# A one-core attention and MLP block: the q weights loaded behind the second chunk of x, two statistics moved ahead, later K products in half rounds, and a new order of the work

## The chip, the cores and the metric

The kernel runs on one core of a Trainium2 chip. The metric is the device time of one execution in microseconds; lower is better. The time before the change is the median of three runs. One further execution was recorded by the profiler, and every duration below comes from that one. The engines are PE (matrix products), ACT, DVE and POOL (elementwise work), and SP, which here only issues transfers.

## The reference

One input x of 2048 rows by 512 columns is normalised per row. From the normalised x an attention with 32 query heads of width 16 and one shared key and value head is computed, and beside it an MLP; the result is x plus their product.

```python
xn = layernorm(x)                              # no scale, no shift, eps 1e-5
q = (xn @ wq) in 32 heads of 16; k = xn @ wk; v = xn @ wv      # one k, one v for all heads
p = softmax(q @ k.T / 4)
s = (p @ v, heads side by side) @ wo
g = silu(silu(xn @ w1) @ w2)                   # w1: 512 x 1792, w2: 1792 x 512
return x + s * g
```

All arrays are bfloat16. B_x is not used.

## The kernel before, in words

The kernel text does not list its instructions. It holds a planner (class Planner) that is run while the program is built: each piece of work is a task or a job with an estimated duration, the planner keeps a clock for each engine, and it places at every step the piece that can start with the best priority. The order so found is the order of each engine's queue; semaphores keep the dependences. On the chip every engine then works through its queue in that order, so an instruction that must wait holds up all that stands behind it.

The rows of x are 16 tiles of 128 rows, in four chunks of four tiles. All times of the planner are in nanoseconds.

**The start.** SP and ACT issue the loads of tiles 0 to 3 one by one, then SP issues wk, wv, wq (512 KB) and the second, third and fourth chunk of x (512 KB each), L482 to L490, in that order. DVE computes the statistics of a tile (L575), gathers them (L579), and writes the normalised tile (L611); ACT does the statistics of tile 1. PE transposes the normalised tile (L650), ACT or DVE copies the transposed tile out of PSUM (L660, L661). In the first chunk the K product (L685) and the first q product (L797) follow tile by tile, then the values (L723). For tiles 4 to 7 the statistics may only be placed once the copy of the transposed tile 3 has been placed (the gate at L578); the statistics of tiles 4 to 11 come together into one group of eight for the reciprocal root (FIRST = (2, 2, 8, 4)). The load of w1 (1792 KB) is issued by SP when tile 5's normalisation has been placed.

**Scores and exponentials.** 32 groups (16 blocks of heads, two halves of each) by 64 score tiles are 2,048 score products (L1033, L1039). Each is four matmuls of 64 rows by 32 columns with 512 moving columns. A score tile goes to one of two places: ACT takes the exponential (L1829, one or two tiles at a time, into pa_sb), or DVE makes an integer in 16 bits that stands for an exponential (L1124, into db_sb), of which POOL makes three shifted copies in batches of eight (L1311, into ds_sb). A tile of ACT needs one product with v, a tile of DVE needs four (L1393). DVE's share may begin only when the keys of 12 tiles are there (DK = 12).

**PE's two lanes.** Most work on PE is done in half rounds: four matmuls of 64 rows, which use half of the array, on lane 0 or lane 1; two half rounds run side by side. Scores, products with v, and the products of the MLP, q and the output (L761) are of this kind (mode "U"). A job of several half rounds does those of one lane first, then those of the other, and all sum into one bank of PSUM. Transposes, values and the K products are full rounds, which use both lanes: mode "F" is a full array, mode "C" four column groups with all 128 rows. A change of mode costs SWITCH = 105 in the plan. The K product of a chunk is four rounds of mode "C" (mk_K); with KU set to 1, a K product of a whole chunk is made a job of half rounds instead:

```python
if KU and n == NQ:
    product(jb, lambda k, rows, a, n: wk2(k, rows), lambda k, rows: xnT_sb[rows, k, ka * P:kb * P],
            lambda k: ["wk", "wv"] + keys)
```

In the main step (pe_step) a half round of a K job goes ahead of scores; on lane 0 other jobs go ahead of products with v, on lane 1 scores go first.

**The price of a transfer.** In Planner.place a load is taken to begin 1.85 us (early) or 1.4 us after its issue, or when the one before is through, to need its bytes divided by 250 per nanosecond, and 0.6 us more.

**The seeds.** The class Mix changes some twenty of the planner's thresholds at random for every 6 us of the plan, by the number that stands for that stretch in SEEDS; 0 keeps the base values. Another list of seeds gives another order of the whole middle. The end (the last output rows) has an order of its own.

Of the kernel before, what the change touches and what calls it, by code (L numbers as in the profile page):

```python
# [15 lines left out]
P = 128  # L16
DH = 16
# [2 lines left out]
W1_AT, SKIP = 5, 1877.999  # L20
T_ISSUE, T_SWDGE = 450.0, 1000.0
J_BASE, J_END, MIXJ = 0.114, 1.312, 2
SEEDS, STRETCH = [0, 621430, 964855, 634377, 64350, 0, 694092, 944034, 510981, 983451, 126593, 580856, 234150, 0, 405364, 0, 0, 639952, 236919, 380010, 794098, 385191, 672036, 0, 789095, 553358, 196796, 902258, 0, 0, 0, 514317, 0, 331162, 593301, 0, 0, 437315, 0, 0, 917832, 457243, 378342, 445316, 218187, 875070, 402692, 608418, 665513, 0, 0, 713570, 834070, 919202, 142859, 159991, 0, 53048, 725479, 111780, 0, 961704, 55976, 234814, 688798, 646486, 6388, 105124, 192922, 681295, 882883, 467008, 979031, 477536, 901050, 975096, 0, 0, 980853, 663567, 0, 620538, 913744, 251242, 618568, 299334, 120371, 0, 397467, 0, 362185, 47491, 718084, 0, 0, 0, 0, 0, 635882, 0, 0, 0, 0, 0, 0, 0, 0, 0, 0], 6000.0
STG = {2: 3, 3: 11}
LOG2E = 1.4426950408889634

# [12 lines left out]
T_TP, T_COLD, N_COLD = 46.0, 427.0, 11  # L39

KA = 0.0
T_V, T_VE, V_KB = 220.0, 410.0, 150

FIRST = (2, 2, 8, 4)
KU, VG_PRIO, ROOM0 = 0, 0, 4
T_SP, T_ST = 600.0, 480.0
FS, T_SQ, T_LD, PR_LD = 4, 210.0, 1500.0, 1

SHIFT = (0.0, 32.0, 64.0, 96.0)
# [4 lines left out]
PE, AC, DV, PO, SP = "PE", "ACT", "DVE", "POOL", "SP"  # L54
# [54 lines left out]
class Planner:  # L109
# [47 lines left out]
    def place(self, eng, dur, emit, reads, writes, dma=0, t0=None, ports=1, after=None):  # L157
        op = Op()
        op.eng, op.emit, op.inc, op.val, op.know, op.sem, op.ports = eng, emit, False, 0, None, None, ports
        deps = self.deps(eng, reads, writes)  # L160
        if after is not None:
            deps.append(after)
        other = self.last2.get(PO if eng == DV else DV) if ports == 2 and eng in self.last2 else None
        if other is not None:
            deps.append(other)
        seen = set()
        op.deps = []
        for d in deps:
            if id(d) not in seen:
                seen.add(id(d))  # L170
                op.deps.append(d)
        if t0 is None:
            t0 = max(self.clk[eng], self.ready(eng, reads, writes), self.locked(eng, ports))
        op.t0 = t0
        op.end = t0 + dur
        if eng in self.last2 and ports == 2:
            self.last2[eng] = op
        op.dma, op.ring = dma, None
        if dma < 0:
            op.vis = self.acc_t = max(op.end - dma, self.acc_t + ACC_GAP)  # L180
        elif dma:
            start = max(t0 + (1850.0 if t0 < 1000.0 else 1400.0), self.dma_t if dma > 1 else 0.0)
            if dma > 1:
                self.dma_t = start + dma / 250.0
            op.vis = start + dma / 250.0 + 600.0
        self.clk[eng] = op.end
        op.idx = len(self.order[eng])
        self.order[eng].append(op)
        self.count += 1
        for k in reads:  # L190
            self.readers.setdefault(k, []).append(op)
        for k in writes:
            self.lastw[k] = op
            self.readers[k] = []
        return op
# [179 lines left out]
def bass_recurrent_scan__grouped_kv_mqa__dense_activation_silu__prompt_kernel(  # L375
# [29 lines left out]
    with ExitStack() as es:  # L405
        def sb(name, shape, dt):
            return es.enter_context(nc.sbuf_tensor(name, shape, dt))
# [3 lines left out]
        wq_sb = sb("wq_sb", [P, NDC, D], BF16)  # L411
        wkv_sb = sb("wkv_sb", [P, NDC, 2 * DH], BF16)
# [39 lines left out]
        def x_tile(t):  # L452
            return ds_sb[:, XB + t // BS, (t % BS) * NQ:(t % BS + 1) * NQ].bitcast(BF16)
# [10 lines left out]
        pl = Planner()  # L464
# [8 lines left out]
        def dma(eng, name, out_, in_, kb, writes, reads=(), prio=1, preds=(), on_place=None):  # L473
            return pl.add(Task(eng, T_ISSUE, lambda e: e.dma_start(out_, in_), reads, writes, prio, preds, on_place,  # L474
                               dma=kb * 1024))

        def xkey(t):
            return ("Ds", XB + t // BS, t % BS)
# [3 lines left out]

        for t in range(4):
            dma((SP, AC)[t % 2], "x", x_tile(t), xv[:, t, :], 128, [xkey(t)], prio=-2)
        dma(SP, "wk", wkv_sb[:, :, 0:DH], A_wk.rearrange("(dc p) e -> p dc e", p=P), 16, ["wk"], prio=0)
        dma(SP, "wv", wkv_sb[:, :, DH:2 * DH], A_wv.rearrange("(dc p) e -> p dc e", p=P), 16, ["wv"], prio=0)
        dma(SP, "wq", wq_sb[:], A_wq.rearrange("(dc p) n -> p dc n", p=P), 512, ["wq"], prio=0)
        for j in range(1, 4):
            dma(SP, "x", ds_sb[:, XB + 4 * j // BS, 4 * j % BS * NQ:(4 * j % BS + 4) * NQ].bitcast(BF16).rearrange("p (t d) -> p t d", d=D),
                xv[:, 4 * j:4 * j + 4, :], 512, [xkey(4 * j + h) for h in range(4)], prio=1)  # L490
        def later(task, which):
# [69 lines left out]
        xn_task, t_done = {}, set()  # L561
# [9 lines left out]
        for j in range(4):  # L571
            for t in range(4 * j, 4 * j + 4):
                if t == 1:
                    continue
                ts_ = pl.add(Task(DV, 593.0, lambda v, t=t: v.bn_stats(stats_sb[:, t, :], x_tile(t)),  # L575
                                  [xkey(t)], [("st", t)], 1 + j,
                                  gate=(lambda j=j: xn_task[STG[j]].op is not None) if j > 1 else
                                  (lambda: ("xnT", 3) in pl.lastw) if j > 0 else None))  # L578
                pl.add(Task(DV, 66.0, lambda v, t=t: v.bn_aggr(mv_sb[:, t, :], stats_sb[:, t, :]),  # L579
                            [("st", t)], [("mv", t)], 1 + j, [ts_]))  # L580
        aggr = {w[1]: task for e in (DV, AC) for task in pl.tasks[e] for w in task.writes if isinstance(w, tuple) and w[0] == "mv"}
# [2 lines left out]
        for n in first:  # L584
# [5 lines left out]
            def dv(fn, reads, writes, pre, ports=1):  # L590
                return pl.add(Task(DV, 66.0, fn, reads, writes, g, [pre] if pre is not None else [], ports=ports))
            if a < FS:
                t = pl.add(Task(AC, T_SQ, lambda q, w=w, a=a, b=b: q.activation(w, mv_sb[:, a:b, 1], ACT.Sqrt, bias=scr_sb[:, 3:4]),
                                [("mv", i) for i in tiles] + ["eps"], [("ve", a)], -1, [aggr[i] for i in tiles] + [eps]))
                if b >= FS:
                    pl.add(Task(AC, T_LD, lambda q: q.activation(scr_sb[:, 0:1], scr_sb[:, 1:2], ACT.Exp), ["scr"], ["scr2"], PR_LD, [t]))
                t = dv(lambda v, y=y, w=w: v.reciprocal(y, w), [("ve", a)], [("rs", a)], t)
            else:
                t = pl.add(Task(DV, 66.0, lambda v, a=a, b=b, w=w: v.tensor_scalar(
                    w, mv_sb[:, a:b, 1], LN_EPS, None, op0=ALU.add), [("mv", i) for i in tiles], [("ve", a)], g,  # L600
                    [aggr[i] for i in tiles], ports=2))
                t = dv(lambda v, y=y, w=w: v.tensor_scalar(
                    y.bitcast(I32), w.bitcast(I32), -0.5, RSQRT_M, op0=ALU.mult, op1=ALU.add), [("ve", a)], [("rs", a)], t, 2)
                for it, (c0, c1) in enumerate(RSQRT_C):
                    t = dv(lambda v, y=y, h=h, c0=c0: v.scalar_tensor_tensor(
                        out=h, in0=y, scalar=c0, in1=y, op0=ALU.mult, op1=ALU.mult), [("rs", a)], [("vh", a)], t)
                    t = dv(lambda v, w=w, h=h: v.tensor_tensor(h, h, w, ALU.mult), [("ve", a), ("vh", a)], [("vh", a)], t)
                    t = dv(lambda v, y=y, h=h, c1=c1: v.scalar_tensor_tensor(
                        out=y, in0=h, scalar=c1, in1=y, op0=ALU.add, op1=ALU.mult), [("rs", a), ("vh", a)], [("rs", a)], t)
# [1271 lines left out]
        while True:  # L1881
            e = min(ENGINES, key=pl.clk.get)
# [12 lines left out]
            t = min([r] + [pl.clk[o] for o in ENGINES if o != e and pl.clk[o] > pl.clk[e]])  # L1895
            if t == INF:
                t = pl.clk[e] + 50.0
# [63 lines left out]
```

## Time and profile before

| what | us |
|---|---|
| median of three runs | 655.4 |
| lowest and highest run | 654.64 and 655.53 |
| the profiled execution, time | 655.33 |
| the profiled execution, span of the core | 653.5 |
| first exponential of a score tile begins | 10.79 |
| POOL's first shifted copies begin | 37.87 |
| PE done with the last dense stretch, about | 645 |

Times in the profile count from the start of the span. A row of the timeline gives the start, the length, the engine, the line, the operation, the tile written and those read, the count of instructions merged, and in brackets the idle time before it and what ended it. PEld is the load of weights, which overlaps PE. SPq is an issue of SP's queue. A row of the stretches gives the stretch, its length, for each of the five engines busy time and count, the granted clock, the DMA share and GB/s.

### The profile page before, as it was taken

What the parts mean: (1) busy time and instruction counts of PE and PEld (TensorE: products, weight loads), DVE (VectorE), ACT (ScalarE), POOL (GpSimd) and SP (SyncE); (2) the same over time, 40 slices, a digit from 0 to 9 for tenths busy, and PEclk for the clock granted to TensorE, in tenths of its full rate; (3) what the DMA queues carried; (4) which work ended last, traced back from release to release, by engine and by line L of the source; (5) the groups of instructions that cost most, each with busy time, mean ns of one, the idle gap of its engine ahead of it and who ended that gap; (6) DMA issues with size and microseconds to landing.
All of it is one profiled execution on the core that took longest, in us unless ns stands there. A gap on an engine that the chain in (4) does not pass through costs nothing.

```text
span 653.5 us, 44343 instructions
## 1 busy us (share of the span) xinstructions
PE 644.5 (99%) x22007; PEld 347.8 (53%) x19480; DVE 632.8 (97%) x1136; ACT 640.9 (98%) x1132; POOL 578.6 (89%) x331
## 2 busy tenths in 40 slices
PE   7999999999999999999999999999999999999997
PEld 3455656555555554554465555545555555475543
DVE  8999999999999999999999999999999999997995
ACT  7999999999999999999999999999999999999996
POOL 3068899999999999999989999999998999997961
PEclk9999999999999999999999999999999999999999
DMA  6521110000011210000000001000000001200001
GB/s 179 157 66 34 38 42 21 11 5 10 13 35 36 37 34 14 10 5 4 11 5 10 13 13 27 4 5 10 6 10 5 10 14 21 51 4 6 4 3 36
DMA packets 12920, 16.57 MB, mean 25 GB/s; under 512 B 2432, under 2 KB 11904, under 8 KB 12544
## 3 DMA queue, kind: packets, MB, share of 16 engines
q1 hardware_dynamic: 10384, 11.31, 5.9%
q0 software_dynamic: 1920, 2.03, 2.3%
q8 instruction: 162, 2.65, 1.7%
q10 hardware_dynamic: 432, 0.39, 0.2%
q14 instruction: 22, 0.18, 0.1%
HBM read 8.95 MB, written 3.67 MB: 19 GB/s over the span
## 4 chain that ended last, share of the span: by engine, by line
PE 96%; DVE 2%; DMA 1%; SPq 0%; issue 0%
PE ps L1393 33%; PE ps L1039 29%; PE ps L761 20%; PE ps L1033 13%; DMA ds_sb<-in_A_x_dram 1%; DVE stats_sb L575 1%; PE ps L650 1%; PE ps L1625 0%; PE ps L685 0%; SPq L474 0%; PE ps L723 0%; DVE w_sb L856 0%; DVE xn_sb L611 0%; DVE mv_sb L579 0%; DVE w_sb L859 0%
## 5 line engine op out<-in xcount | busy, mean ns | idle before, releaser
L1829 ACT ACTIVATE pa_sb<-ps 128x512 bf16<-128x512 f32 (+1 forms) x1039 | 608.6, 771 | 2.7 <-PE ps L1039 1.9
L1311 POOL INT64_ADD ds_sb<-db_sb x299 | 563.7, 1958 | 33.4 <-PE ps L1393 12.4
L1124 DVE TENSOR_SCALAR db_sb<-ps 128x512 uint16<-128x512 f32 x794 | 494.8, 682 | 6.3 <-PE ps L1039 3.7
L1039 PE MATMUL ps<-qt_sb,kt_sb 64*32 64x512 bf16 x5664 | 481.4, 378 | 1.0 <-ACT pa_sb L1829 0.6
L1393 PE MATMUL ps<-ds_sb,v_sb 64*32 64x512 bf16 x4872 | 359.4, 376 | 0.0
L1393 PE MATMUL ps<-pa_sb,v_sb 64*32 64x512 bf16 x2472 | 258.0, 377 | 0.0
L1033 PE MATMUL ps<-qt_sb,kt_sb 64*32 64x512 bf16 x2528 | 244.2, 375 | 0.8 <-DMA qt_sb<-qt_sb 0.5
L1039 PEld LDWEIGHTS ps<-qt_sb,kt_sb 64*32 64x32 bf16 x5664 | 136.3, 89 | 150.0 <-ACT pa_sb L1829 65.4
L1393 PE MATMUL ps<-db_sb,v_sb 64*32 64x512 bf16 x1624 | 189.5, 376 | 0.0
L1393 PEld LDWEIGHTS ps<-ds_sb,v_sb 64*32 64x32 bf16 x4872 | 140.6, 91 | 41.8 <-issue 12.1
L761 PE MATMUL ps<-xnT_sb,w_sb 64*32 64x512 bf16 x1792 | 133.7, 377 | 0.4 <-issue 0.4
L761 PE MATMUL ps<-w_sb,u_sb 64*32 64x512 bf16 x1792 | 132.7, 377 | 0.0
L1393 PEld LDWEIGHTS ps<-pa_sb,v_sb 64*32 64x32 bf16 x2472 | 87.9, 91 | 28.2 <-issue 10.2
L1393 PEld LDWEIGHTS ps<-db_sb,v_sb 64*32 64x32 bf16 x1624 | 62.1, 91 | 13.0 <-issue 3.4
L761 PEld LDWEIGHTS ps<-xnT_sb,w_sb 64*32 64x32 bf16 x1792 | 44.2, 91 | 24.4 <-issue 6.0
L761 PEld LDWEIGHTS ps<-w_sb,u_sb 64*32 64x32 bf16 x1792 | 44.5, 91 | 17.3 <-issue 4.0
L817 ACT ACTIVATE t_sb<-ps 128x512 bf16<-128x512 f32 x72 | 48.8, 677 | 0.6 <-PE ps L761 0.5
L818 DVE SCALAR_TENSOR_TENSOR u_sb<-t_sb,ps 128x512 bf16<-128x512 bf16 x56 | 38.0, 679 | 0.6 <-ACT t_sb L817 0.2
L761 PE MATMUL ps<-xnT_sb,wq_sb 64*32 64x512 bf16 x480 | 36.1, 377 | 0.0
L761 PE MATMUL ps<-wo_sb,on_sb 64*32 64x512 bf16 x384 | 29.4, 377 | 0.0
L1414 DVE STREAM_TRANSPOSE ps<-ps 128x512 f32<-128x512 f32 (+1 forms) x33 | 23.2, 707 | 4.3 <-PE ps L1393 2.7
L1450 POOL DMA_DIRECT2D kt_sb<-kt_sb x4 | 2.3, 584 | 21.3 <-DVE kt_sb L703 16.0
(79 smaller groups left out, 197.0 us busy)
## 6 DMA issues: line engine op xcount, KB each, us to landing
w_sb<-in_B_w_dram SPq DMA_DIRECT2D x1, 1792.0 KB, 8.9
w_sb<-in_B_w_dram SPq DMA_DIRECT2D x14, 128.0 KB, 2.5
ds_sb<-in_A_x_dram SPq DMA_DIRECT2D x3, 512.0 KB, 6.5
qt_sb<-qt_sb SPq DMA_DIRECT2D x16, 96.0 KB, 2.1
out_dram<-in_A_x_dram SPq DMA_DIRECT2D x12, 128.0 KB, 2.5
out_dram<-ob_sb POOLq DMA_DIRECT2D x12, 128.0 KB, 3.1
v_sb<-v_sb SPq DMA_DIRECT2D x8, 80.0 KB, 2.2
wq_sb<-in_A_wq_dram SPq DMA_DIRECT2D x1, 512.0 KB, 4.6
```

Of the source, the lines that this page charges most:

```text
L575: ts_ = pl.add(Task(DV, 593.0, lambda v, t=t: v.bn_stats(stats_sb[:, t, :], x_tile(t)), [xkey(t)], [("st", t)], 1 + j, gate=(lambda j=j: x ...
L650: h = pe.transpose(dst[:, k, dc * P:(dc + 1) * P], xn_sb[:, t % 4, dc * P:(dc + 1) * P], ident[:, :])
L761: h = pe.matmul(bank(b)[32 * j:32 * (j + 1), :], lhsT=lhs(k, rows, 32 * j, 32), rhs=rhs(k, rows), start=first, stop=last, tile_position=(r ...
L817: t1 = Task(AC, T_AF + 0.8333 * NQ, lambda a: a.activation(t_sb[:, k, :], bank(b), ACT.Tanh, scale=scale), [("ps", b)], [("t", k)], 0)
L818: t2 = Task(DV, T_P, lambda v: v.scalar_tensor_tensor(out=dst, in0=t_sb[:, k, :], scalar=1.0, in1=bank(b), op0=ALU.add, op1=ALU.mult), [(" ...
L1033: h = pe.add_instruction(mybir.InstMatmult(name=pe.bass.get_next_instruction_name(), engine=mybir.EngineType.PE, ins=[pe.lower_ap(q), pe.l ...
L1039: h = pe.matmul(to, lhsT=keys, rhs=q, start=True, stop=True, tile_position=(r0, 32 * j), skip_group_check=True)
L1124: bt.P[k] = pl.add(Task(DV, T_P, lambda v: v.tensor_scalar(db_sb[:, bt.b, k * NQ:(k + 1) * NQ], bank(b), 128.0 * LOG2E, 128.0 * (SHIFT_BET ...
L1311: whole["po"].append(pl.add(Task(PO, 100.0 + (T_P64 - 100.0) * bt.n / BS, lambda g: g.int64_add(ds_sb[:, s, 0:n].bitcast(U64), db_sb[:, bt ...
L1393: h = pe.matmul(bank(OB)[q:q + 32, :], lhsT=lhs(rows), rhs=rhs[rows], start=s0, stop=s1, tile_position=(64 * l, q), skip_group_check=True)
L1414: t1 = pl.add(Task(DV, (T_TR - 60.0) / parts + 60.0, lambda v, cols=cols: v.transpose(bank(OB)[:, cols], bank(OB)[:, cols]), [("ps", OB)], ...
L1829: op = pl.place(AC, 0.8333 * NQ * n + T_AF, lambda a: a.activation(pa3[:, k0:k1 + 1:max(1, k1 - k0), :], ps3[:, b0:b1 + 1:step, :], ACT.Ex ...
```

## The change

Five things are changed. The load of wq is issued behind the load of the second chunk of x, no longer ahead of it. The statistics of tiles 4 and 5 may be placed once the normalised tile 3 has been placed, without waiting for the copy of the transposed tile 3. KU is 1, so the K products of chunks 1 to 3 are jobs of half rounds. The planner's prices of transfers are changed (bytes per nanosecond 360 for 250, wk and wv counted as 216 KB each, the two copies of v as 200 KB each). And the list of seeds is another one, so all of the order is found anew. The sizes of the transfers themselves stay as they were.

```diff
-SEEDS, STRETCH = [0, 621430, 964855, ...
+SEEDS, STRETCH = [0, 841236, 442622, ...
-T_V, T_VE, V_KB = 220.0, 410.0, 150
+T_V, T_VE, V_KB = 220.0, 410.0, 200
-KU, VG_PRIO, ROOM0 = 0, 0, 4
-T_SP, T_ST = 600.0, 480.0
+KU, VG_PRIO, ROOM0 = 1, 0, 4
+T_SP, T_ST, DMA_RATE, W_KB, WQ_AT, EARLY_ST = 600.0, 480.0, 360.0, 216, 2, 6
-                self.dma_t = start + dma / 250.0
-            op.vis = start + dma / 250.0 + 600.0
+                self.dma_t = start + dma / DMA_RATE
+            op.vis = start + dma / DMA_RATE + 600.0
-        dma(SP, "wk", wkv_sb[:, :, 0:DH], A_wk.rearrange("(dc p) e -> p dc e", p=P), 16, ["wk"], prio=0)
-        dma(SP, "wv", wkv_sb[:, :, DH:2 * DH], A_wv.rearrange("(dc p) e -> p dc e", p=P), 16, ["wv"], prio=0)
-        dma(SP, "wq", wq_sb[:], A_wq.rearrange("(dc p) n -> p dc n", p=P), 512, ["wq"], prio=0)
+        dma(SP, "wk", wkv_sb[:, :, 0:DH], A_wk.rearrange("(dc p) e -> p dc e", p=P), W_KB, ["wk"], prio=0)
+        dma(SP, "wv", wkv_sb[:, :, DH:2 * DH], A_wv.rearrange("(dc p) e -> p dc e", p=P), W_KB, ["wv"], prio=0)
         for j in range(1, 4):
+            if j == WQ_AT:
+                dma(SP, "wq", wq_sb[:], A_wq.rearrange("(dc p) n -> p dc n", p=P), 512, ["wq"], prio=1)
...
-                                  (lambda: ("xnT", 3) in pl.lastw) if j > 0 else None))
+                                  (lambda t=t: ("xnT", 3) in pl.lastw or t < EARLY_ST and xn_task[3].op is not None) if j > 0 else None))
```

More of the change, by code (lines that the diff above doesn't have):

```diff
@@ L22 @@
 J_BASE, J_END, MIXJ = 0.114, 1.312, 2
-SEEDS, STRETCH = [0, 621430, 964855, 634377, 64350, 0, 694092, 944034, 510981, 983451, 126593, 580856, 234150, 0, 405364, 0, 0, 639952, 236919, 380010, 794098, 385191, 672036, 0, 789095, 553358, 196796, 902258, 0, 0, 0, 514317, 0, 331162, 593301, 0, 0, 437315, 0, 0, 917832, 457243, 378342, 445316, 218187, 875070, 402692, 608418, 665513, 0, 0, 713570, 834070, 919202, 142859, 159991, 0, 53048, 725479, 111780, 0, 961704, 55976, 234814, 688798, 646486, 6388, 105124, 192922, 681295, 882883, 467008, 979031, 477536, 901050, 975096, 0, 0, 980853, 663567, 0, 620538, 913744, 251242, 618568, 299334, 120371, 0, 397467, 0, 362185, 47491, 718084, 0, 0, 0, 0, 0, 635882, 0, 0, 0, 0, 0, 0, 0, 0, 0, 0], 6000.0
+SEEDS, STRETCH = [0, 841236, 442622, 405335, 567912, 314118, 873438, 0, 627131, 798395, 635206, 352442, 876084, 0, 845192, 878658, 715361, 0, 0, 0, 0, 929392, 0, 147357, 834836, 0, 843404, 82997, 87583, 0, 183416, 475187, 328250, 20514, 324735, 579026, 575682, 405081, 0, 0, 413202, 322195, 431036, 0, 484529, 63499, 233030, 0, 717291, 470758, 0, 817057, 677992, 201789, 396322, 0, 470246, 5121, 721216, 297895, 780396, 826273, 40344, 738000, 424892, 651759, 0, 845596, 816191, 150562, 368306, 536650, 883608, 27708, 553900, 665892, 581120, 391376, 0, 0, 809747, 402390, 666337, 413840, 945857, 570728, 808506, 0, 541665, 55374, 255585, 45267, 0, 862883, 0, 0, 0, 0, 0, 0, 0, 0, 0, 798084, 0, 0, 0, 0, 0], 6000.0
 STG = {2: 3, 3: 11}
```

## Prediction

> **What bounds the kernel now.** I read the page first (busy shares, chain that ended last), then the busy time by stretches of 100 us, then the timeline of the first 36 us with its chain, and last the waits and DMA landings there. From the page:
>
> ```profile
> span 653.5 us, 44343 instructions
> PE 644.5 (99%) x22007; PEld 347.8 (53%) x19480; DVE 632.8 (97%) x1136; ACT 640.9 (98%) x1132; POOL 578.6 (89%) x331
> PE 96%; DVE 2%; DMA 1%; SPq 0%; issue 0%
> L1829 ACT ACTIVATE pa_sb<-ps 128x512 bf16<-128x512 f32 (+1 forms) x1039 | 608.6, 771 | 2.7 <-PE ps L1039 1.9
> L1124 DVE TENSOR_SCALAR db_sb<-ps 128x512 uint16<-128x512 f32 x794 | 494.8, 682 | 6.3 <-PE ps L1039 3.7
> ```
>
> The reader is to see three engines filled to within 1 to 3% and a chain that runs through PE for 96% of the span. DVE and DMA have the other 3%, nearly all of it at the start. Outside the start, then, the time is PE's number of matmuls times their spacing. The spacing stands in the stretches of 100 us:
>
> ```profile
> 100.00:200.00 100.00, 100.00 (x3584) 56.73 (x3145) 99.72 (x173) 100.00 (x177) 99.01 (x54) 1.00 0.05 15
> 200.00:300.00 100.00, 99.62 (x3536) 53.73 (x3168) 99.44 (x172) 99.50 (x187) 97.45 (x55) 1.00 0.11 22
> 300.00:400.00 100.00, 100.00 (x3520) 52.71 (x3048) 98.77 (x167) 99.90 (x174) 96.71 (x55) 1.00 0.06 11
> 400.00:500.00 100.00, 100.00 (x3553) 52.81 (x3176) 99.35 (x170) 99.99 (x184) 96.08 (x53) 1.00 0.04 8
> 500.00:600.00 100.00, 99.73 (x3501) 56.61 (x3084) 95.03 (x164) 99.53 (x178) 92.94 (x52) 1.00 0.09 17
> ```
>
> PE's count is the first bracket of a row (PE is the second entry, behind the length). The work is issued in half rounds of four 64-row matmuls, two lanes side by side: 17,694 matmuls in 500 us are 113.0 ns for a half round, 111.6 in the best stretch and 114.2 in the worst, at a granted clock of 1.00 throughout. PE counts as busy all the time, yet its density differs by over 2% from stretch to stretch. The order of the work alone makes that difference, and the change draws the whole order anew.
>
> Now the start. PE cannot be filled there, for the work comes late. The timeline:
>
> ```profile
> 2.68 0.51 SPq L474 DMA_DIRECT2D wq_sb<-in_A_wq_dram  x1
> 3.23 1.64 SPq L474 DMA_DIRECT2D ds_sb<-in_A_x_dram  x3
> 6.67 0.74 DVE L611 TENSOR_SCALAR xn_sb<-ds_sb,mv_sb,rstd_sb 128x512 bf16<-128x512 bf16 x2
> 7.57 0.76 DVE L661 COPY xnT_sb<-ps 128x512 bf16<-128x512 bf16 x2 [0.17 <-PE ps L650]
> 8.55 1.11 PE L797 MATMUL ps<-xnT_sb,wq_sb 128*32 128x128 bf16 x64
> 8.79 1.29 DVE L575 BATCH_NORM_STATS2 stats_sb<-ds_sb 128x6 f32<-128x512 bf16 x2 [0.47 <-DMA ds_sb<-in_A_x_dram]
> 10.79 3.47 ACT L1829 ACTIVATE pa_sb<-ps 128x512 bf16<-128x512 f32 x6 [0.50 <-PE ps L1039]
> 13.64 17.80 ACT L1829 ACTIVATE pa_sb<-ps 128x512 bf16<-128x512 f32 x27
> 16.75 1.38 DVE L611 TENSOR_SCALAR xn_sb<-ds_sb,mv_sb,rstd_sb 128x512 bf16<-128x512 bf16 x4
> 17.52 0.37 SPq L474 DMA_DIRECT2D w_sb<-in_B_w_dram  x1
> ```
>
> The second chunk of x comes last for DVE (8.79, idle 0.47 before it). From there DVE works without a pause through eight statistics to the normalised tiles (16.75), which release the transposes, the K product of chunk 1 and the load of w1 (17.52). ACT's exponentials run without a pause from 10.79 to 31.44. Two rows of the chain and of the DMA landings give the transfers:
>
> ```profile
> 3.23 5.54 DMA ds_sb<-in_A_x_dram
> w_sb<-in_B_w_dram SPq DMA_DIRECT2D x1, 1792.0 KB, 8.9
> wq_sb<-in_A_wq_dram SPq DMA_DIRECT2D x1, 512.0 KB, 4.6
> ```
>
> wq lands at 2.68 + 4.6 = 7.28, the second chunk at 3.23 + 5.54 = 8.77. Both are 512 KB, and they follow each other by 1.49 us.
>
> **The change part by part.** All sums are against the profiled execution, 655.33 us (span 653.5), 0.07 below the median of the three runs, 655.4.
>
> 1. The q weights behind the second chunk. Two issues of SP change places, of the same size, so nothing is added on its queue, and the third and fourth chunks keep their places. The second chunk lands at about 7.28 and wq at about 8.77.
>
> 2. Two statistics ahead. DVE ends the last normalised tile at 6.67 + 0.74 = 7.41. One statistic, now landed, goes in at once, where DVE waited 0.17 and then 0.47. The DVE chain up to the load of w1 thus comes up to 0.64 us earlier: 0.64 is the upper end, nothing is the lower (the landing may slip past 7.41 by as much). I take 0.64, since the two landings trade places and the size is the same.
>
> 3. What that delays. The two copies of the transposed tiles stand behind that statistic: 1.29 us for two with the aggregate between them, about 0.65 for one, so they end at about 7.41 + 0.65 + 0.76 = 8.82 in place of 8.33. The q product, which began at 8.55, waits for wq until 8.77 at the least. The first exponential follows it, so 0.2 to 0.5 us later. It costs little at the end: ACT loses a part of one exponential of 0.6 us, and PE had gaps there. Bounds 0 and +0.5; I take +0.1, nearest to what one lost score half round (0.11) is worth.
>
> 4. Later K products in half rounds. Now each is a block of full rounds for both lanes. The timeline around the second and the third of the three:
>
> ```profile
> 25.50 0.40 PE L1039 MATMUL ps<-qt_sb,kt_sb 64*32 64x512 bf16 x4
> 25.83 1.05 PE L685 MATMUL ps<-xnT_sb,wkv_sb 128*32 128x512 bf16 x16
> 26.80 0.40 PE L761 MATMUL ps<-xnT_sb,w_sb 64*32 64x512 bf16 x4
> 32.32 0.40 PE L1039 MATMUL ps<-qt_sb,kt_sb 64*32 64x512 bf16 x4
> 32.65 1.05 PE L685 MATMUL ps<-xnT_sb,wkv_sb 128*32 128x512 bf16 x16
> 33.71 0.39 PE L1393 MATMUL ps<-pa_sb,v_sb 64*32 64x512 bf16 x1
> 35.49 0.39 PE L1033 MATMUL ps<-qt_sb,kt_sb 64*32 64x512 bf16 x4
> 35.92 0.39 PE L1033 MATMUL ps<-qt_sb,kt_sb 64*32 64x512 bf16 x4
> ```
>
> On one lane half rounds follow at about 0.215 us (35.92 - 35.49 = 0.43 for two). From the end of the last half round (its start and 0.215) to the next start the block takes 26.80 - 25.72 = 1.08 and 33.71 - 32.54 = 1.17 us of both lanes. Eight half rounds on two lanes are 8 x 0.215 / 2 = 0.86. So 0.22 to 0.31 each, three of them 0.8 if PE were full at all three. It is full at the third only; the first two lie in the stretch that ACT holds, so where PE alone counts the gain is 0.3 to 0.8. One cost speaks the other way: the half rounds of one lane must end before the other lane's begin, so a product takes 2 x 0.86 = 1.7 us in place of about 1.0, and the keys of chunk 2, which must be there before DVE's share of the exponentials may begin, come 0.7 later. That is covered by the exponentials ACT has in hand (27 in a row); without the cover it would be +0.7. Range -0.8 to +0.7, taken at -0.75 (0.31 and twice 0.22), nearest the rows, since each block holds both lanes whatever ACT does.
>
> The Trainium skill, TensorEngine Tiling (Array Packing), section Key Properties, says that a change of tiling mode drains the engine. The gaps of 0.11 us on the way in (25.72 to 25.83, 32.54 to 32.65) agree with it. The same page under Restrictions and Gotchas says that different row tiles cannot use one PSUM bank at once, which speaks against half rounds; the row at 26.80 shows four matmuls of one bank and two row halves done in 0.40 us in all, so the measurement decides, and by the page each K product would cost some 0.9 us more instead.
>
> 5. The plan's prices. DMA bytes are priced at 360 for 250, the wk and wv loads at 216 KB for 16, the copies of v at 200 for 150. They move nothing on the chip by themselves, but they say where in PE's queue the first round on w1 stands. Old: 1.4 + 7.34 + 0.6 = 9.3 us behind its issue; new: 1.4 + 5.10 + 0.6 = 7.1. The row has 8.9. PE waited for it already once:
>
> ```profile
> PEld ps L761 <- DMA w_sb<-in_B_w_dram: 0.4, 1, 0.4
> ```
>
> Bounds: nothing (the round stands behind other work) to +2.2, the difference of the two prices. I take nothing, because K half rounds go ahead of that round in the plan's code; the rest is the second rival.
>
> 6. New order. The five stretches have a standard deviation of 32 matmuls, 0.9%, so 0.9 us in 100; over six such stretches, if independent, 2.2 us. A redraw may cost or gain that much, or 2.8 at the ends of 8 in 10. I take 0. It also redraws how many of the 2,048 score tiles go to ACT; one that moves from DVE to ACT saves PE six matmuls (four products on v become one), 6 x 28 ns = 0.17 us.
>
> Sum: -0.64 + 0.1 - 0.75 + 0 + 0 = -1.29, hence **654.0** from 655.33. The earlier load of w1 is the same 0.64, counted once.
>
> **The rivals.**
>
> A. The new order is looser. At 114.2 ns for a half round in every stretch, as in the worst row, the 600 us of the middle would take 6 us more; from half a nanosecond more per half round (2.7 us) the time is clearly slower than before. Price 2.2 to 4.2, time 656.2 to 658.2, say 657.0. For it: nothing in the start outweighs a change of 0.5% in the middle. Against: the old order has stretches as loose already.
>
> B. The first round on w1 stands too early in PE's queue. PE then waits up to 2.2 us more, and scores behind it starve ACT. The stretch ahead of that round, in the table by stretches:
>
> ```profile
> 24.00:25.00 1.00, 1.00 (x20) 0.55 (x13) 1.00 (x4) 1.00 (x3) 0.00 (x0) 1.00 0.57 152
> 25.00:26.00 1.00, 1.00 (x16) 0.23 (x13) 0.93 (x5) 1.00 (x2) 0.00 (x0) 1.00 0.38 88
> ```
>
> PE starts 36 matmuls there in 2 us, where the middle has 71, so I let gaps absorb a third of the wait: +1.4, time 654.0 + 1.4 = 655.4, as before. For it: the price of 7.1 us against a landing of 8.9. Against: ACT has scores in hand, and the order decides.
> The Trainium skill, DMA: Bandwidth & Descriptors, section Anatomy of one DMA, gives 2.0 us plus bytes at 436 GB/s, by which w1 would land 6.2 us behind its issue (an estimate from that page) and B could not happen; the row with 8.9 us differs, and it decides, so B keeps its chance.
>
> C. The change does not do what it says: the second chunk lands no earlier than DVE is free, or the copies' delay takes it all back, and K gains only at its third place. Then -0.3, time 655.0.
>
> D. The new order is tighter, or gives ACT a dozen tiles more (12 x 0.17 = 2.0): 654.0 - 2.2 = 651.8.
>
> **How the numbers follow.** Forecast 0.38, A 0.22, B 0.10, C 0.07, D 0.23. What a measurement of this kernel can tell from no change is about 0.2%, 1.3 us, so faster is below 654.1 and slower above 656.7. Faster: all of D and somewhat over half of the forecast's case, which reaches from 652.8 to 655.3, with a little from C: 0.47. Slower: most of A and some of B's upper end: 0.25. Within: 0.28. The range leaves out one in ten on each side: 654.0 less 3.1 is 650.9 (D with a further 1.0), and 657.3 holds the larger half of A.
>
> **What would show it.** In the changed profile: wq landing after the second chunk; a statistic between the last normalised tile and the copies, with DVE's idle of 0.64 gone and w1 issued at about 16.9 in place of 17.52; the first exponential at 11.0 to 11.3; no full-height K blocks behind the first chunk; a wait for w1 of under 0.5 us at the first round on it (B: over 1.5). The order shows in the count of matmuls per 100 us and in the counts of L1829 and L1124. I would be wrong if the middle moved by over 1%, or if the start lost more at the first exponentials than DVE gained.

## The result and the profile after

| | median, us | lowest to highest | runs |
|---|---|---|---|
| before | 654.88 | 653.86 to 655.53 | 9 |
| changed | 657.18 | 655.58 to 658.59 | 9 |

The ratio is 1.0037 with a 95% interval of 1.0025 to 1.0049: the change makes the kernel slower, by 2.4 us. The forecast was 654.0 and faster; the time lies just within the range, on the other side. The changed kernel scatters more (3.0 us between its runs, 1.7 before), and the execution that was profiled is its slowest, 658.59 us.

First the page of the changed kernel: the span, the engines, the shares of the chain that ended last, the exponentials of ACT and of DVE, and the load of w1.

```profile
span 656.7 us, 44430 instructions
PE 646.5 (98%) x22055; PEld 350.9 (53%) x19495; DVE 631.3 (96%) x1139; ACT 642.1 (98%) x1142; POOL 579.7 (88%) x332
PE 95%; DMA 2%; DVE 1%; ACT 0%; issue 0%; ACTq 0%
...
L1830 ACT ACTIVATE pa_sb<-ps 128x512 bf16<-128x512 f32 (+1 forms) x1049 | 609.8, 760 | 5.0 <-PE ps L1040 3.8
L1125 DVE TENSOR_SCALAR db_sb<-ps 128x512 uint16<-128x512 f32 x802 | 499.4, 679 | 7.9 <-PE ps L1040 2.2
...
w_sb<-in_B_w_dram SPq DMA_DIRECT2D x1, 1792.0 KB, 9.0
```

PE has 48 matmuls more than before, and that is the half rounds alone: three K products of 32 matmuls where there were 16. The chain went through DMA for 1% of the span and now does for 2%; all else has stayed. The counts of L1830 (1049 for 1039) and L1125 (802 for 794) are of instructions, which take one tile or two. In tiles ACT has 862 single ones and 187 pairs, before 842 and 197, which is 1236 both times, so the division of the exponentials is the same. So the first place to look is a transfer. The stretches that hold the start, the next 60 us and the middle, before and then after (length, PE busy and count, then the other engines, the clock, DMA):

```profile
0.00:40.00 40.00, 35.80 (x724) 16.08 (x656) 36.65 (x117) 35.16 (x63) 10.00 (x22) 1.00 0.48 145
40.00:100.00 60.00, 60.00 (x2100) 34.67 (x1864) 59.63 (x102) 59.81 (x105) 54.03 (x29) 1.00 0.17 45
100.00:640.00 540.00, 539.35 (x18992) 292.89 (x16757) 528.97 (x900) 538.92 (x958) 513.28 (x282) 1.00 0.07 14
```

```profile
0.00:40.00 40.00, 34.34 (x739) 15.75 (x675) 35.07 (x115) 33.46 (x55) 7.96 (x21) 1.00 0.52 158
40.00:100.00 60.00, 59.95 (x2074) 34.66 (x1843) 59.45 (x103) 60.00 (x110) 54.62 (x30) 1.00 0.13 36
100.00:640.00 540.00, 539.41 (x18952) 294.14 (x16700) 529.58 (x905) 538.18 (x966) 515.05 (x282) 1.00 0.07 14
```

A matmul of the middle costs 539.35 / 18992 = 28.4 ns. Up to 100 us, less the 48, the changed kernel has done 739 + 2074 - 48 = 2765 matmuls against 724 + 2100 = 2824. It is 59 behind, 1.7 us, before the middle begins. In the first 40 us ACT is busy for 33.46 us where it was for 35.16. (Its counts, 55 and 63, mix exponentials of one and of two tiles and cannot be compared.) The middle loses another 40 matmuls, 1.1 us, in this execution; a second execution, below, does not show that.

The start, from the timeline of the changed kernel:

```profile
2.68 0.51 SPq L474 DMA_DIRECT2D ds_sb<-in_A_x_dram  x1
3.23 0.54 SPq L474 DMA_DIRECT2D wq_sb<-in_A_wq_dram  x1
...
7.36 1.28 DVE L576 BATCH_NORM_STATS2 stats_sb<-ds_sb 128x6 f32<-128x512 bf16 x2
8.56 0.74 DVE L662 COPY xnT_sb<-ps 128x512 bf16<-128x512 bf16 x2
...
10.92 3.41 ACT L1830 ACTIVATE pa_sb<-ps 128x512 bf16<-128x512 f32 x5 [0.50 <-PE ps L1040]
14.32 0.49 DVE L732 TENSOR_TENSOR v_sb<-ps,wj_sb 128x320 bf16<-128x320 f32 x1 [0.46 <-PE ps L724]
16.55 1.38 DVE L612 TENSOR_SCALAR xn_sb<-ds_sb,mv_sb,rstd_sb 128x512 bf16<-128x512 bf16 x4
17.31 0.38 SPq L474 DMA_DIRECT2D w_sb<-in_B_w_dram  x1
24.06 0.74 DVE L704 TENSOR_SCALAR kt_sb<-ps,part_sb 128x512 bf16<-128x512 f32 x1
26.32 0.10 PEld L762 LDWEIGHTS ps<-xnT_sb,w_sb 64*32 64x32 bf16 x4 [1.51 <-DMA w_sb<-in_B_w_dram]
26.32 0.40 PE L762 MATMUL ps<-xnT_sb,w_sb 64*32 64x512 bf16 x4 [1.00 <-DMA w_sb<-in_B_w_dram]
26.56 0.38 PE L762 MATMUL ps<-xnT_sb,wkv_sb 64*32 64x512 bf16 x4
28.78 0.75 DVE L704 TENSOR_SCALAR kt_sb<-ps,part_sb 128x512 bf16<-128x512 f32 x1 [2.10 <-PE ps L762]
```

The chain at that place:

```profile
16.55 0.75 DVE xn_sb L612 x2
17.31 8.96 DMA w_sb<-in_B_w_dram
...
26.32 0.40 PE ps L762 x4
```

w1 is issued at 17.31, 0.21 earlier than before, and lands 8.96 us later, at 26.27. The first round on it stands so early in PE's queue that PE's weights wait 1.51 us for it and its matmuls 1.00; before the change only the weights waited, 0.42. Behind that round in the queue stands the K product of chunk 2, which needs nothing of w1: it begins at 26.56, and DVE, which waits 2.10 us for it, begins to write the keys of chunk 2 at 28.78. (The times of keys, here and below, are the starts of these rows of DVE.) Before the change the same row stood here:

```profile
21.30 0.74 DVE L703 TENSOR_SCALAR kt_sb<-ps,part_sb 128x512 bf16<-128x512 f32 x1
26.93 0.75 DVE L703 TENSOR_SCALAR kt_sb<-ps,part_sb 128x512 bf16<-128x512 f32 x1
...
37.87 5.62 POOL L1311 INT64_ADD ds_sb<-db_sb  x3 [2.55 <-DVE db_sb L1124]
```

The keys of chunk 1 were there at 21.30 for 24.06, those of chunk 2 at 26.93 for 28.78, and POOL's first shifted copies began at 37.87; after the change they begin at 39.88, 2.01 us later:

```profile
39.88 5.62 POOL L1312 INT64_ADD ds_sb<-db_sb  x3 [1.68 <-DVE db_sb L1125]
```

That start of POOL is a mark of how far the start has come; runs 9 and 10 have orders of their own.

### The profile page after: what moved, and what is told of

Same layout as the page of the kernel before. It is cut to its first block, busy times and chain, and to the rows that moved or that the text cites. A ratio compares the mean times of both kernels' runs of the same rounds, so it can differ in the third digit from the quotient of the medians.

```text
span 656.7 us, 44430 instructions
## 1 busy us (share of the span) xinstructions
PE 646.5 (98%) x22055; PEld 350.9 (53%) x19495; DVE 631.3 (96%) x1139; ACT 642.1 (98%) x1142; POOL 579.7 (88%) x332
## 4 chain that ended last, share of the span: by engine, by line
PE 95%; DMA 2%; DVE 1%; ACT 0%; issue 0%; ACTq 0%
PE ps L1394 35%; PE ps L1040 27%; PE ps L762 20%; PE ps L1034 12%; DMA w_sb<-in_B_w_dram 1%; PE ps L1626 1%; DMA ds_sb<-in_A_x_dram 0%; DMA qt_sb<-qt_sb 0%; PE ps L724 0%; ACT L597 0%; DVE stats_sb L576 0%; DVE w_sb L857 0%; PE ps L651 0%; PE ps L798 0%; ACT qt_sb L807 0%
## 5 line engine op out<-in xcount | busy, mean ns | idle before, releaser
L1830 ACT ACTIVATE pa_sb<-ps 128x512 bf16<-128x512 f32 (+1 forms) x1049 | 609.8, 760 | 5.0 <-PE ps L1040 3.8
L1125 DVE TENSOR_SCALAR db_sb<-ps 128x512 uint16<-128x512 f32 x802 | 499.4, 679 | 7.9 <-PE ps L1040 2.2
L1394 PE MATMUL ps<-ds_sb,v_sb 64*32 64x512 bf16 x4872 | 353.4, 377 | 0.0
L1394 PE MATMUL ps<-db_sb,v_sb 64*32 64x512 bf16 x1624 | 184.1, 377 | 0.0
L1394 PEld LDWEIGHTS ps<-ds_sb,v_sb 64*32 64x32 bf16 x4872 | 137.6, 91 | 45.7 <-issue 11.6
L762 PE MATMUL ps<-xnT_sb,w_sb 64*32 64x512 bf16 x1792 | 137.3, 377 | 1.1 <-DMA w_sb<-in_B_w_dram 1.0
L762 PE MATMUL ps<-w_sb,u_sb 64*32 64x512 bf16 x1792 | 135.7, 377 | 0.0
L1394 PEld LDWEIGHTS ps<-db_sb,v_sb 64*32 64x32 bf16 x1624 | 60.1, 91 | 16.9 <-issue 6.0
```

The lines of the kernel that those rows point to most:

```text
L762: h = pe.matmul(bank(b)[32 * j:32 * (j + 1), :], lhsT=lhs(k, rows, 32 * j, 32), rhs=rhs(k, rows), start=first, stop=last, tile_position=(r ...
L1125: bt.P[k] = pl.add(Task(DV, T_P, lambda v: v.tensor_scalar(db_sb[:, bt.b, k * NQ:(k + 1) * NQ], bank(b), 128.0 * LOG2E, 128.0 * (SHIFT_BET ...
L1394: h = pe.matmul(bank(OB)[q:q + 32, :], lhsT=lhs(rows), rhs=rhs[rows], start=s0, stop=s1, tile_position=(64 * l, q), skip_group_check=True)
L1830: op = pl.place(AC, 0.8333 * NQ * n + T_AF, lambda a: a.activation(pa3[:, k0:k1 + 1:max(1, k1 - k0), :], ps3[:, b0:b1 + 1:step, :], ACT.Ex ...
```

## The experiments

Two theories. **S (start):** the time is lost before 40 us, above all at the first round on w1, which the new prices of transfers put ahead of the landing; from there PE is full and the loss comes out at the end one for one. **M (middle):** the new order of the whole is looser, and the start matters little. Every ratio below is to runs of before on the same chip. Six kernels move the load of w1 or its first rounds in the finished queues and leave the order else as it is; one makes the change of the start alone, one is the changed kernel once more, and two let the planner work with other prices.

**1. The load of w1 earlier, in the changed kernel.** It keeps only the waits of the copy of v ahead of it on SP.

```diff
+ w.deps = [d for d in sp[10].deps]      # w: the load of w1; sp[10]: the second copy of v
```

> The changed kernel with the same order on every engine; only the load of w1 is issued right behind the two copies of v of chunk 0 (about 16.0 us, landing about 25.0) and waits for nothing, so that PE's first round on w1 finds its data. Theory S (the loss is made in the start: the plan prices transfers too cheaply, so that round stands 3.5 us too early and PE waits there): the wait of 1.0 to 1.5 us goes and the time falls by 1.0 to 1.5 below the changed kernel's 657.2, to 655.7 to 656.2. Theory M (the loss is made in the middle, the new order is looser): the wait goes, but the time stays within 0.5 of 657.2.

Measured: 657.13 us (12 runs) beside 655.36 for before; ratio 1.0024 (1.0009 to 1.0040). Its timeline:

```profile
15.78 0.59 SPq L474 DMA_DIRECT2D w_sb<-in_B_w_dram  x1
25.09 0.40 PE L762 MATMUL ps<-xnT_sb,w_sb 64*32 64x512 bf16 x4 [0.52 <-DMA w_sb<-in_B_w_dram]
27.56 0.75 DVE L704 TENSOR_SCALAR kt_sb<-ps,part_sb 128x512 bf16<-128x512 f32 x1 [1.11 <-PE ps L762]
```

The issue is 1.53 us earlier, and the keys of chunk 2 are 1.22 earlier, though PE still waits 0.52. In microseconds the time is what M expected, but before was slower on this chip too, 655.36 for 654.88. By the ratio it is 1.6 us over before, between S (0.8 to 1.3 over) and M (1.8 to 2.8). It settles nothing: the interval overlaps the changed kernel's.

**2. The first rounds on w1 later, in the changed kernel.** Their load stays; the first four half rounds on w1 stand behind the K product of chunk 2.

```diff
+ first, k2 = [q[i0], q[i0 + 2], q[i0 + 4], q[i0 + 6]], q[i0 + 17]    # q: PE's queue, i0: the first round on w1
+ for o in first:
+     q.remove(o)
+ at = q.index(k2) + 1
+ q[at:at] = first
```

> The changed kernel with one thing moved in PE's queue: the first four half rounds on w1 stand behind the K product of chunk 2 and not among it. No other engine's order is touched. Theory S: K of chunk 2 and the scores in between no longer wait for w1, the keys of chunk 2 come about 2 us earlier than 28.8, and the time falls by 0.7 to 1.5, to 655.7 to 656.5. Theory M: no more than 0.4 is gained.

Measured: 658.77 us (6 runs); ratio 1.0053 (1.0035 to 1.0071), no gain, though in its profile PE waits for w1 nowhere and the keys of chunk 2 come 1.74 us earlier:

```profile
27.04 0.75 DVE L704 TENSOR_SCALAR kt_sb<-ps,part_sb 128x512 bf16<-128x512 f32 x1 [0.54 <-PE ps L762]
```

A miss for S. The interval holds the changed kernel's ratio, so a gain of 1 us is not seen although the wait is gone; run 7 comes back to it.

**3. The control: before, with w1 late.** The load also waits for a DVE instruction of about 19 us in the plan.

```diff
+ w.deps = w.deps + [first instruction of DVE with t0 > 19000]
```

> The kernel before with the same order on every engine; the load of w1 waits for one more instruction of DVE and is issued about 2.4 us later (about 19.9), so that PE stands about 2 us before its first round on w1. Theory S: slower than before by 1.3 to 2.2 us (656.2 to 657.1), the lag is never made up. Theory M: PE makes most of it up in the gaps behind, slower by less than 0.6.

Measured: 656.47 us (12 runs); ratio 1.0016 (1.0004 to 1.0027), so +1.0 us, between the two expectations.

```profile
19.98 0.37 SPq L474 DMA_DIRECT2D w_sb<-in_B_w_dram  x1
27.95 0.40 PE L761 MATMUL ps<-xnT_sb,w_sb 64*32 64x512 bf16 x4 [0.94 <-DMA w_sb<-in_B_w_dram]
```

With the old order untouched, a wait of 0.94 us of PE at this place costs 1.0 us at the end, with an interval of 0.3 to 1.8 us. What S says of the place is so; that the loss comes out one for one fits, but the interval is too wide to show it.

**4. Parts 1 and 2 alone.** Before, with wq issued behind the second chunk and the two statistics ahead of the copies.

```diff
+ sp[4], sp[5] = sp[5], sp[4]
+ q[37:41] = q[39:41] + q[37:39]          # DVE's queue
```

> The kernel before with the order of all else kept: wq issued behind the second chunk of x, and the statistics of tiles 4 and 5 ahead of the two copies of the transposed tiles on DVE. This is parts 1 to 3 of the prediction alone, which gave -0.5 (654.4 from 654.9). Theory S now: the chain of DVE gains 0.2 us at w1's issue and the first exponential loses 0.1, so -0.2 to +0.3. Theory M: nothing, 654.9.

Measured: 655.51 us (12 runs); ratio 1.0003 (0.9990 to 1.0016): no change that can be told from nothing. The interval, -0.7 to +1.0 us, still holds the prediction's -0.5, so it is the trace that speaks:

```profile
7.53 1.29 DVE L575 BATCH_NORM_STATS2 stats_sb<-ds_sb 128x6 f32<-128x512 bf16 x2
...
10.80 0.62 DVE L703 TENSOR_SCALAR kt_sb<-ps,part_sb 128x384 bf16<-128x384 f32 x1 [0.66 <-PE ps L685]
...
17.68 0.37 SPq L474 DMA_DIRECT2D w_sb<-in_B_w_dram  x1
```

DVE's 0.64 us of idle time ahead of the statistics is gone, and 0.66 of it stands again ahead of the first keys, where DVE waits for PE: the copies came later, so the K product did too. w1 is issued at 17.68, not earlier than before.

**5. w1 on POOL's queue, without a wait, in the changed kernel.**

```diff
+ sp.remove(w)
+ w.eng, w.deps = PO, []
+ po.insert(at, w)                        # behind POOL's first copy of keys
```

> The changed kernel with the same order on PE, DVE and ACT; the load of w1 is issued by POOL right behind its first copy of keys (about 12.7 us), waits for nothing and has landed before PE reaches its first round on it. So the wait for w1 is gone altogether, where the earlier run only shortened it. Theory S (the loss is made in the start): at 30 us PE is about 2 us further than in the changed kernel, and the time is 655.0 to 656.0, within 0.15% of before. Theory M (the middle is looser): 656.5 to 657.2.

Measured: 660.09 us (6 runs) beside 654.81; ratio 1.0084 (1.0067 to 1.0102). Both theories missed it.

```profile
12.74 0.84 POOL L474 DMA_DIRECT2D w_sb<-in_B_w_dram  x1
...
21.64 0.40 PE L1394 MATMUL ps<-pa_sb,v_sb 64*32 64x512 bf16 x4 [2.77 <-DMA v_sb<-v_sb]
23.37 0.61 PE L1040 MATMUL ps<-qt_sb,kt_sb 64*32 64x512 bf16 x4
...
27.71 0.40 PE L762 MATMUL ps<-xnT_sb,w_sb 64*32 64x512 bf16 x4
```

The wait for w1 is gone (27.71), but the copies of v, issued by SP at 14.86, now come after the large load that was issued ahead of them (it lands 8.5 us after its issue, at 21.2), and PE waits 2.77 us for them. Then the clock falls; the stretches of the same kernel (PE alone):

```profile
22.00:23.00 1.00, 1.00 (x38) 0.89 0.07 16
23.00:24.00 1.00, 1.00 (x32) 0.50 0.00 0
24.00:25.00 1.00, 1.00 (x19) 0.50 0.00 0
25.00:26.00 1.00, 1.00 (x16) 0.50 0.61 137
```

The granted clock is 0.50 for about 3.4 us (0.80 on average from 26.00 to 26.50, where it comes back), and a row of four matmuls takes 0.61 us in place of 0.40. So this run does not price w1, but it shows a larger loss in the start coming out in the time. POOL's mark stands at 41.92, 2.2 us later than in the next kernel, and the time is 660.09 - 656.95 = 3.1 us longer.

**6. The changed kernel again**, on the chip of run 5.

> The changed kernel itself, as it is, beside the run without the wait on the same chip. Both theories: 0.25% to 0.5% over before, 656.5 to 658.5; it is the bar that the other run is held against.

Measured: 656.95 us (9 runs); ratio 1.0045 (1.0029 to 1.0060). Its stretches:

```profile
0.00:40.00 40.00, 35.20 (x743) 16.14 (x679) 35.50 (x115) 33.58 (x56) 8.15 (x21) 1.00 0.51 158
40.00:100.00 60.00, 59.97 (x2078) 34.64 (x1848) 59.46 (x103) 60.00 (x111) 54.65 (x30) 1.00 0.13 37
100.00:640.00 540.00, 539.78 (x19004) 290.58 (x16740) 529.82 (x906) 539.45 (x968) 516.77 (x283) 1.00 0.07 14
```

Up to 100 us it is 743 + 2078 - 48 = 2773 against 2824, 51 matmuls or 1.4 us behind, as the first execution was (59). In the middle it has 19,004, 12 more than before, where the first execution had 40 fewer. So the 40 that were missing in the middle of the first execution are not the order's: the 52 between two executions of one program (1.5 us) are scatter. That scatter is as large as what M claims, so two executions cannot refute M either; the count over all runs follows run 8.

**7. Edits 1 and 2 together, in the changed kernel.**

```diff
+ w.deps = [d for d in sp[10].deps]
+ first, k2 = [q[i0], q[i0 + 2], q[i0 + 4], q[i0 + 6]], q[i0 + 17]
...
+ q[at:at] = first
```

> The changed kernel with both edits: w1 issued right behind the copies of v (about 16.0), and the first four half rounds on w1 moved behind the K product of chunk 2. PE then waits for w1 nowhere, and the copies of v are not disturbed. Theory S (the loss is made before 30 us): at 30 us PE is 1.5 to 2 us further than in the changed kernel, and the time is 655.0 to 656.0. Theory M (the rest of the new order is looser as well): 656.3 to 657.

Measured: 655.59 us (11 runs) beside 654.88; ratio 1.0015 (1.0006 to 1.0025), as S expected and under M. The timeline, then the stretches:

```profile
16.24 0.59 SPq L474 DMA_DIRECT2D w_sb<-in_B_w_dram  x1
...
26.95 0.75 DVE L704 TENSOR_SCALAR kt_sb<-ps,part_sb 128x512 bf16<-128x512 f32 x1
```

```profile
0.00:40.00 40.00, 36.15 (x759) 17.22 (x695) 36.21 (x116) 34.26 (x57) 8.73 (x21) 1.00 0.52 158
40.00:100.00 60.00, 60.00 (x2087) 33.39 (x1848) 59.48 (x103) 60.00 (x110) 54.70 (x30) 1.00 0.14 39
100.00:640.00 540.00, 539.99 (x19016) 292.94 (x16752) 530.13 (x907) 539.77 (x969) 516.60 (x283) 1.00 0.06 14
```

No wait for w1 is left, the keys of chunk 2 are there at 26.95, 1.83 earlier and where they were before the change (26.93), and up to 100 us the count is 759 + 2087 - 48 = 2798, 26 behind in place of 51 to 59. The whole middle stands in the same order as in the changed kernel. By the ratios the two edits give back 0.22 to 0.30% of 654.9, 1.4 to 2.0 us of the 2.4 to 2.9. The interval does not overlap that of run 6 and meets that of the first comparison only at its edge. But by the counts only 25 to 33 matmuls of it, 0.7 to 0.9 us, were won before 100 us. The rest is not on view before 100 us; it came in the middle, where both have the same order. Run 2 shows the same from the other side: at 100 us it is 759 + 2084 - 48 = 2795, 29 behind, as far as this run, and its time is 1.0053.

**8. The other control: before, with w1 early**, by the edit of run 1.

> The kernel before with its order; only w1 is issued right behind the copies of v of chunk 0 and waits for nothing (about 16.1 for 17.5). Control for the runs with an earlier w1: before waits for w1 only 0.4 us of a weight load, so both theories expect -0.3 to +0.2 (654.5 to 655.0); a gain of over 0.6 would say that an earlier w1 helps by itself.

Measured: 654.55 us (11 runs); ratio 0.9993 (0.9984 to 1.0002). Where PE does not wait for w1, an earlier w1 gives nothing. What the earlier load wins in the changed kernel is thus the wait, not the earlier load as such.

**Where the ten executions stand.** Ten of the profiled executions have one of two orders behind the start: that of before, or that of the changed kernel. For each, the matmuls that it is behind the first profile of before at 100 us, those from 100 to 640 us, and the ratio of its kernel (many executions, not this one alone):

| kernel | behind at 100 us | 100 to 640 us | ratio |
|---|---|---|---|
| before | 0 | 18,992 | 1 |
| run 3 (w1 late) | 61 | 19,001 | 1.0016 |
| run 4 (start alone) | 4 | 18,984 | 1.0003 |
| run 8 (w1 early) | 24 | 18,988 | 0.9993 |
| changed | 59 | 18,952 | 1.0037 |
| run 6 (changed again) | 51 | 19,004 | 1.0045 |
| run 1 (wait 0.52) | 13 | 18,952 | 1.0024 |
| run 2 (no wait) | 29 | 18,964 | 1.0053 |
| run 7 (no wait) | 26 | 19,016 | 1.0015 |
| run 5 (w1 on POOL) | 121 | 18,988 | 1.0084 |

The wait shows in the first column. Where it is shortened or gone (runs 1, 2 and 7), the changed kernel is 22 to 46 matmuls further at 100 us, 0.6 to 1.3 us. Run 1, which still waits 0.52 us, is the furthest of them, so other things in the start scatter as well. The second column is where M would show. The new order has 18,979 on average, the old 18,991, so 12 fewer or 0.3 us, well inside the scatter; but its six executions spread over 64 matmuls (1.8 us), the four of the old order over 17 (0.5 us). By these counts M as a loss of 2 us is not borne out, a part of it is not excluded, and why the new order scatters more is open.

**9. The planner with prices nearer to the traces**, the change else kept. 360 bytes per nanosecond only for loads issued in the first 5 us, 250 after that, the first loads to begin 2.3 us behind their issue, w1 counted as 2050 KB; some of the seeds are others, since the plan was made anew.

```diff
+ rate = DMA_RATE if t0 < 5000.0 else 250.0
- start = max(t0 + (1850.0 if t0 < 1000.0 ...
+ start = max(t0 + (2300.0 if t0 < 1000.0 ...
- op.vis = start + dma / DMA_RATE + 600.0
+ op.vis = start + dma / rate + 600.0
- w1 ... 1792
+ w1 ... 2050
```

> The changed kernel with the plan's prices put nearer to what the traces show: 360 only for the loads of the first 5 us, which begin 2.3 us behind their issue, 250 for all later transfers, w1 counted as 2050 KB; and with a list of seeds found anew for these prices. wq behind the second chunk, the early statistics and the K products in half rounds stay. Its plan ends PE's work 2.7 us later than that of the changed kernel (648.9 for 646.2). Theory S: the plan is later but true, so the chip keeps to it and the time is 656.5 to 657.5, as the changed kernel or better. Theory M: the time follows the plan, 659 to 660.

Measured: 657.01 us (5 runs); ratio 1.0036 (1.0024 to 1.0048), S's number and not M's. The planner's own clock, which the kernel text gives when it is run, ends PE's work at 648.94 here and at 646.24 in the changed kernel. It is 2.7 us worse in the plan and the same on the chip, so the better plan of the change did not carry over. That its promise rested on transfers that do not land when it says fits this, but the seeds differ too, so it is not shown apart. Nor is this kernel better than the changed one; one reason on view is that a wait came again at another copy:

```profile
43.23 0.39 PE L1395 MATMUL ps<-pa_sb,v_sb 64*32 64x512 bf16 x1 [0.75 <-DMA v_sb<-v_sb]
43.71 2.65 ACT L1831 ACTIVATE pa_sb<-ps 128x512 bf16<-128x512 f32 x5 [0.47 <-PE ps L1041]
44.63 1.22 DVE L1860 TENSOR_SCALAR db_sb<-ps 128x1024 uint16<-128x1024 f32 x1 [1.01 <-PE ps L1035]
```

A copy of v issued at about 39.5, behind four more loads of weights, holds PE for 0.75 us, and ACT and DVE stand 0.47 and 1.01 us behind it. Up to 100 us the count is 777 + 2044 - 48 = 2773, 51 behind, as in run 6.

**10. The same with K products in full rounds** (KU = 0, seeds of its own; its plan ends PE's work at 649.04).

```diff
-KU, VG_PRIO, ROOM0 = 1, 0, 4
+KU, VG_PRIO, ROOM0 = 0, 0, 4
```

> The same with KU = 0, the later K products as full rounds again, and seeds of its own; its plan ends PE's work at 649.0, 0.1 later than the run with half rounds. The prediction's part 4 (half rounds save 0.75) says 0.7 slower than that run. Theory S says that half rounds bring nothing in the start, where the other lane has no work and transposes and values drain PE anyway: within 0.4 of it, 656.6 to 657.6.

Measured: 657.21 us (6 runs); ratio 1.0038 (1.0024 to 1.0051). Between two plans that end 0.1 us apart, half rounds and full rounds cannot be told apart. What follows is bounded: the intervals are 1.6 and 1.8 us wide, so a gain of 0.75 is not excluded, only not seen.

## Why the prediction was wrong, point by point

- **What bounds the kernel.** Right in the three full engines. That losses are made only in the start is shown for the wait for w1; for the rest of the loss it is not. The reading that the order alone makes the density of a stretch was wrong. The order of the changed kernel had 18,952 to 19,016 matmuls from 100 to 640 us in six executions, so a part of the spread that priced step 6 and two rivals can be scatter from one execution to the next.
- **Steps 1 and 2, the early statistics (-0.64).** The second chunk is there in time (statistics at 7.36 without a wait), and the idle time that I named is gone. The step failed in what comes of it. Two statistics went ahead of the copies, not one, so the copies came at 8.56 (7.57 before), and DVE waits later, 0.46 us for the first values (14.32) in the changed kernel, 0.66 for the first K product in run 4. The normalised tiles are 0.20 earlier in the changed kernel, and w1 is issued 0.21 earlier, not 0.64; in run 4 it is not issued earlier at all, and no gain is seen. The step stopped at DVE; where the stall goes next should have been asked of PE, whose K product follows the copies.
- **Step 3, what that delays (+0.1).** The first exponential is at 10.92 for 10.79, a smaller delay than the 0.2 to 0.5 given. What it costs at the end was not measured apart.
- **Step 4, half rounds (-0.75).** Not found. That the keys of chunk 2 come later was seen, 0.7 by the working; they came 1.85 later, of which run 7 takes back all with w1 out of the way. Chunk 1's came 2.8 later, which the working had not asked about, and run 7 leaves that as it was. Run 10 sees no gain, though it does not exclude one of 0.75.
- **Step 5, the prices (0). This is the step that failed most plainly: a wait was put at nothing that costs about 1 us.** The working had the price of 7.1 us beside a landing of 8.9, and set it aside "because K half rounds go ahead of that round in the plan's code". They do not hold each other back: the rule looks at one lane at a time, and the rounds on w1 stood on the other lane, beside K's. The plan takes w1 as issued at 15.7 and landed 7.1 us later, at 22.8 on its own clock; the chip issues it at 17.31 and has it at 26.27. Over all runs the landing took 7.7 to 9.3 us, never 7.1. So the wait of rival B came, with its mark (over 1.5 us, on the weights), and as PE's queue is worked in order, it held the K product and DVE behind it. What the wait costs: 1.00 us of PE's time in the trace, 0.6 to 1.3 us by the counts at 100 us, and 1.0 us (0.3 to 1.8) at the end for 0.94 us of wait in run 3. The rival's price of +1.4 was near that and its chance of 0.10 too low; its time of 655.4 rested on 1.3 us of gains that steps 2 and 4 did not bring. Nor does this step alone turn the sign: without the wait (run 7) the kernel is still slower than before. The 6.2 us that the prediction works out for w1 rest on a fit that the Trainium skill (DMA: Bandwidth & Descriptors, Anatomy of one DMA) gives for loads that GpSimd issues, while SP issued this one; from POOL's queue (GpSimd) in run 5 it took 8.5 us, so the figure falls short there as well.
- **Step 6 and rival A, the order.** The forecast of 0 for the middle is not refuted: 18,979 matmuls on average over six executions against 18,991 over four. Rival A's time of 657.0 came true, and that was luck at least for the 1 us of the wait, which is not A's reason.
- **What stays open.** Of the 2.4 us the wait explains about 1. With the wait gone, run 7 is still 1.0 us slower than before (0.4 to 1.6), and run 2, which is as far at 100 us and has the same order behind it, is 3.5 us slower (2.3 to 4.7). So what comes behind 100 us in the new order differs by some 2.5 us between two kernels that are alike up to there (they ran on two chips), and no run says why. Run 7 is 26 matmuls behind at 100 us, 0.7 us, and chunk 1's keys are late in it; but run 8, in the old order, is 24 behind with no loss, so that does not explain it. At the end DVE waits 4.4 us for PE once where it waited 1.6 before; what stands behind that wait takes no longer (8.3 us for 8.6).

## What to carry to other kernels

In an order that is written down ahead, the price of a transfer is no estimate of time but a decision on what stands behind it. Compare every priced landing with the landing in the trace, and where the price is shorter, look which instruction is the first to need the data and what is queued behind that instruction on all its lanes. A saving found at a waiting engine counts only when the next instruction that would wait has been followed through the other engines as well. And before a spread between stretches is called the order's, the same program should be profiled twice.

## What the runs showed of the hardware

- **After a pause of 2.77 us the clock was halved for a while.** In run 5 PE stood idle from about 18.9 to 21.64, and from about 22.8 to 26.2 its granted clock was 0.50. The changed kernel's pauses at this place, 0.55 and 1.00 us, left it at 1.00. The Trainium skill, TensorE: Matmul & The Clock Gate, Part 1, says that a window of 3.4 us which has been idle halves the clock until a busy one has passed. The 3.4 us at 0.50 agree with the window. The idle time is shorter than that, and PE had worked again for over 1 us when the clock fell. If the last work before the pause, a transpose of 0.62 us at 18.25, does not count as work, the idle time is 3.3 us. The run does not show whether it counts, nor whether a shorter pause is enough.
- **A large load delays small copies of another queue.** In run 5 w1 was on POOL's queue, the copies of v on SP's, and the copies still came behind it: the first two took 6.4 us from issue to landing (the median), where they took 2.2 in the changed kernel.
- **Scatter.** Two executions of one program had 18,952 and 19,004 matmuls in the same 540 us, 1.5 us of work, at a clock of 1.00 in both. Over six executions of the changed order the spread was 64 matmuls, over four of the old order 17.
